# Transposing V on VectorE in a decode attention block with gradients: 32x32 blocks, block-diagonal score weights, and small products on ScalarE

## Chip, cores, metric

One Trainium2 chip, one core. The metric is the device time of that core in microseconds, as the median of several executions. An execution over 1.5% above the fastest of its kernel counts as slow, the others as fast. Engines: PE is the matrix engine, PEld its weight loads, DVE is VectorE, ACT is ScalarE, POOL is GpSimd, SP issues the transfers (SPq is its queue).

## The reference

A decode block for one token, forward and backward: layer norm, attention over a cache (32 query heads, 32 KV heads, 8192 positions, 128 per head), plus a gated MLP. Outputs are the block's output and the gradients of x, both caches and all weights.

```python
q = (xn @ wq).reshape(B, Sq, Hq, Dh)                      # xn = layernorm(x); D = 640
scores = jnp.einsum("bhqd,bhkd->bhqk", q, k) * Dh ** -0.5
p = softmax(scores)
o = jnp.einsum("bhqk,bhkd->bhqd", p, v)
out = x + o.reshape(B, Sq, Hq * Dh) @ wo + (silu(xn @ w1) * (xn @ w3)) @ w2
# ... outputs: out, and jax.vjp(...)(grad_out): dx, dK, dV, dwq, dwo, dw1, dw3, dw2
```

Per head the kernel loads K and V (2 MB each) and stores dK and dV (2 MB each): 32 heads are 268 of the 303.5 MB that are moved. dV is the outer product of p with the row `do` = wo·g, and dK the outer product of U = p·(do·V + const) with q. So a head needs the scores q·K, the softmax, then do·V, then a dot product, and only then may dK be formed.

## The kernel before

One head, in the order in which the instructions are issued. `T` transposes a 128x512 fp32 piece (pairs of bf16 taken as one fp32) with four PE transposes and copies it out of PSUM on ACT. `Mp` takes the score sums from two such pieces. `ev` and `selm` bring the sums to positions on partitions.

```python
def T(h, kind, c):
    W3 = kv_tiles[(kind, h)][:].bitcast(F32).rearrange("p (i w) -> p i w", w=P)
    pT = pst()
    for k in range(4):
        nc.tensor.transpose(pT[:, k * P:(k + 1) * P], W3[:, 4 * c + k, :], ident_f[:])
    KT = kt_tile()
    nc.scalar.copy(KT[:].rearrange("p k w -> p (k w)"), pT[:])
    hd[h]["kt"][(kind, c)] = KT

def Mp(h, kind, c0):
    # ... 4 matmuls, weights 128x32 (one column tile for each piece), 128x512 moving

def head(h):
    # ...
    if has_prev:
        outers_a(h - 1)          # V: two outer products, store dV; K: the first half
    for c in range(had, NCH, 2):
        T(h, "K", c); T(h, "K", c + 1)
        if c >= 2: Mp(h, "K", c - 2)
        # ...
    T(h, "V", 0); T(h, "V", 1)
    Mp(h, "K", NCH - 2); ev(h, "K")
    T(h, "V", 2); T(h, "V", 3)
    selm(h, "K"); mx(h)          # row maximum over 64 positions (DVE)
    # ... further V pieces between: mx_bc (maximum over partitions), expo, zsum
    probs(h)                     # 1/sum, P2 (DVE), Z (DVE)
    if has_prev:
        outers_b(h - 1)          # K: the second half, store dK
    # ... T(h, "V", 7), side work, weights and rows of head h + 1
    T(h + 1, "K", 0); T(h + 1, "K", 1)
    Mp(h, "V", NCH - 2); ev(h, "V")
    o_sum(h)                     # 16 matmuls p·V
    selm(h, "V"); rdot(h)        # dot product on DVE
    T(h + 1, "K", 2)
    dsum(h)                      # its broadcast by PE, then U2 and Z on DVE
    T(h + 1, "K", 3); Mp(h + 1, "K", 0)
    dq_sum(h)                    # 16 matmuls U·K
```

Loads and stores share one queue, in program order; ten buffers of 2 MB rotate. A store gives its buffer back and at once asks for the next load, which goes out only with three buffers free:

```python
def load_next():
    if not pending or len(free_slots) < lag[0]:      # lag[0] = 3 after the start
        return
    kind, h = pending.pop(0)
    t = free_slots.pop(0)
    fifo(t[:], (kc if kind == "K" else vc)[h])        # nc.sync queue
    # ...
def store(kind, h):
    t = kv_tiles.pop((kind, h))
    # ...
    fifo((dkc if kind == "K" else dvc)[h], t[:])
    free_slots.append(t)
    load_next()
```

The MLP is computed between heads 1 and 2. While it runs, K and V of heads up to 5 are asked for.

## Time and profile before

| | before |
|---|---|
| time, median of 3 | 730.84 us (730.36 to 731.22) |
| span of the profiled run, mean granted PE clock | 729.3 us, 0.928 |
| moved | 303.5 MB, 416 GB/s over the span |

The first part of the page gives each engine's busy time and share of the span; the fourth, the chain of work that ended last, followed back from the last instruction and summed by engine.

```profile
PE 600.8 (82%) x5186; PEld 375.4 (51%) x5193; DVE 461.3 (63%) x811; ACT 375.8 (52%) x727; POOL 28.2 (4%) x43
...
DMA 55%; PE 34%; DVE 6%; ACT 2%; issue 1%; SPq 0%; ACTq 0%; DVEq 0%
```

PE is the busiest engine, but more than half of the chain lies in transfers. That, and the full DMA row which the prediction quotes, make this a kernel at the DMA's limit with an engine not far below it.

### The profile page before, as it was taken

To read this page: it belongs to the slowest core of one execution; us is meant where nothing else is said; L and a number is where in the kernel's file an instruction comes from. 1 tells how busy PE (TensorE), PEld (TensorE's weight loads), DVE (VectorE), ACT (ScalarE), POOL (GpSimd) and SP (SyncE) were. 2 spreads that over 40 slices of the span, in tenths; PEclk is the share of its full clock that TensorE was granted. 3 is DMA by queue.
4 is the path that set the end of the run, shared out by engine and by line. 5 is a ranking of instruction groups with operands and counts; after the bars stand their busy time and mean duration, and the time that the engine had idled before them with its cause. 6 is when DMAs were issued, how large, how long until landed. Compare 5 with 4: busy or idle time off the path is not lost.

```text
span 729.3 us, 12905 instructions
## 1 busy us (share of the span) xinstructions
PE 600.8 (82%) x5186; PEld 375.4 (51%) x5193; DVE 461.3 (63%) x811; ACT 375.8 (52%) x727; POOL 28.2 (4%) x43
## 2 busy tenths in 40 slices
PE   4989589999999989887897798877897878977930
PEld 2556366665566556554454454544564545544520
DVE  4179646677868886676466755655746765667482
ACT  3740736665666566554465554554564555645510
POOL 0010100000100000001000000000000000000000
PEclk9996799999999999999999999998999999999965
DMA  8999999999999999999999999999999999999994
GB/s 353 404 411 422 427 427 428 417 426 426 414 417 426 430 426 426 428 428 428 422 428 430 428 425 428 427 428 429 424 429 425 430 429 430 428 427 430 430 396 161
DMA packets 28005, 303.53 MB, mean 416 GB/s; under 512 B 2804, under 2 KB 5304, under 8 KB 11304
## 3 DMA queue, kind: packets, MB, share of 16 engines
q1 hardware_dynamic: 22518, 277.70, 90.1%
q0 software_dynamic: 5408, 24.99, 8.4%
q8 instruction: 41, 0.67, 0.4%
q14 instruction: 20, 0.16, 0.1%
q10 hardware_dynamic: 18, 0.01, 0.0%
HBM read 151.34 MB, written 151.34 MB: 415 GB/s over the span
## 4 chain that ended last, share of the span: by engine, by line
DMA 55%; PE 34%; DVE 6%; ACT 2%; issue 1%; SPq 0%; ACTq 0%; DVEq 0%
DMA kv<-in_A_v_cache_dram 21%; DMA out_dram<-kv 18%; PE pT L318 16%; DMA kv<-in_A_k_cache_dram 14%; PE sA L339 5%; PE dA L339 3%; PE X L433 3%; DVE kv L466 3%; PE m L356 2%; DMA wo_g<-in_A_wo_dram 2%; PE gu_ps L556 1%; ACT KT L320 1%; PE dh_ps L567 1%; DVE wq_g L521 1%; PE acc L199 1%
## 5 line engine op out<-in xcount | busy, mean ns | idle before, releaser
L320 ACT COPY KT<-pT 128x512 f32<-128x512 f32 x512 | 287.9, 587 | 230.0 <-PE pT L318 210.3
L318 PE MATMUL pT<-ident_f,kv 128*128 128x128 f32 x2048 | 306.0, 288 | 62.5 <-DMA kv<-in_A_k_cache_dram 35.3
L318 PEld LDWEIGHTS pT<-ident_f,kv 128*128 128x128 f32 x2048 | 235.4, 148 | 155.1 <-PE pT L318 50.0
L466 DVE TENSOR_TENSOR kv<-qd,U 128x4096 bf16<-128x4096 bf16 x64 | 146.1, 2285 | 0.0
L466 DVE TENSOR_TENSOR kv<-qd,P 128x4096 bf16<-128x4096 bf16 x64 | 143.6, 2285 | 0.0
L433 PE MATMUL X<-kv,Z 128*32 128x512 bf16 x1024 | 95.2, 407 | 1.8 <-DVE Z L450 1.8
L339 PE MATMUL dA<-KT,qz 128*32 128x512 bf16 x512 | 83.5, 405 | 0.0
L339 PE MATMUL sA<-KT,qz 128*32 128x512 bf16 x512 | 83.5, 406 | 0.0
L416 DVE SCALAR_TENSOR_TENSOR U<-m,P 128x64 bf16<-128x64 f32 x32 | 7.5, 234 | 87.2 <-PE m L356 87.2
L382 DVE TENSOR_REDUCE mrow<-m 128x1 f32<-128x64 f32 x32 | 7.2, 224 | 69.6 <-PE m L356 69.5
L433 PEld LDWEIGHTS <-Z 128*32 128x32 bf16 x1024 | 33.0, 100 | 34.5 <-issue 7.1
L339 PEld LDWEIGHTS <-qz 128*32 128x32 bf16 x1024 | 29.6, 95 | 40.5 <-issue 38.0
L356 PE MATMUL m<-selc,KT 64*128 64x64 f32 x256 | 30.5, 242 | 7.9 <-ACT KT L346 7.8
L356 PEld LDWEIGHTS m<-selc,KT 64*128 64x128 f32 x256 | 21.5, 144 | 29.9 <-ACT KT L346 20.0
L376 ACT CAST qd<-pT 128x256 bf16<-128x256 f32 x32 | 11.9, 372 | 40.3 <-DVE kv L466 31.6
L389 DVE TENSOR_REDUCE negM<-m 128x1 f32<-128x128 f32 x32 | 9.3, 292 | 33.0 <-PE m L386 33.0
L521 DVE SCALAR_TENSOR_TENSOR wq_g<-wq_g,side 128x512 bf16<-128x512 bf16 x40 | 27.3, 683 | 0.0
L257 DVE SCALAR_TENSOR_TENSOR side<-wo_g,g_bc 128x640 bf16<-128x640 bf16 x32 | 26.2, 820 | 0.7 <-DMA wo_g<-in_A_wo_dram 0.3
L448 DVE SCALAR_TENSOR_TENSOR U<-m,P 128x128 bf16<-128x128 f32 x32 | 11.4, 355 | 16.4 <-PE m L446 16.4
L406 DVE RECIPROCAL rZ<-m 128x1 f32<-128x1 f32 x32 | 5.3, 167 | 24.1 <-PE m L400 24.1
L346 ACT COPY KT<-dA 64x512 f32<-64x512 f32 x32 | 18.6, 582 | 2.9 <-PE dA L339 2.9
L346 ACT COPY KT<-sA 64x512 f32<-64x512 f32 x32 | 18.5, 579 | 2.0 <-PE sA L339 1.7
(161 smaller groups left out, 372.2 us busy)
## 6 DMA issues: line engine op xcount, KB each, us to landing
out_dram<-kv SPq DMA_DIRECT2D x64, 2048.0 KB, 31.0
kv<-in_A_k_cache_dram SPq DMA_DIRECT2D x32, 2048.0 KB, 26.3
kv<-in_A_v_cache_dram SPq DMA_DIRECT2D x32, 2048.0 KB, 26.3
wq_g<-in_A_wq_dram POOLq DMA_DIRECT2D x7, 640.0 KB, 13.4
wo_g<-in_A_wo_dram POOLq DMA_DIRECT2D x7, 640.0 KB, 19.1
out_dram<-wo_g POOLq DMA_DIRECT2D x7, 640.0 KB, 11.9
out_dram<-wq_g POOLq DMA_DIRECT2D x7, 640.0 KB, 13.4
kv<-in_B_w_dram SPq DMA_DIRECT2D x2, 1728.0 KB, 29.2
```

The source lines that it names most:

```text
L257: nc.vector.scalar_tensor_tensor(junk[:], G_["wo"][:, hh, :], 1.0, g_bc[:], ALU.mult, ALU.mult, accum_out=G_["do"][:, hh:hh + 1])
L318: nc.tensor.transpose(pT[:, k * P:(k + 1) * P], W3[:, 4 * c + k, :], ident_f[:])
L320: nc.scalar.copy(KT[:].rearrange("p k w -> p (k w)"), pT[:])
L339: nc.tensor.matmul(S_[kind][q:q + QW, :], lhsT=S_["qz"][:, o:o + QW], rhs=KTb[c][:, par, :], start=(c0 == 0 and par == 0), stop=(c0 == NCH ...
L346: nc.scalar.copy(XS[0:QH].rearrange("p k w -> p (k w)"), S_.pop(kind)[0:QH, :])
L356: nc.tensor.matmul(S_["m"][:, b0:b0 + 4 * J].rearrange("p (x c k t) -> p k x c t", x=4, k=4, t=2)[:, k], lhsT=XS[0:QH, k, :], rhs=selc[0:Q ...
L376: nc.scalar.copy(qd[:].rearrange("p a d -> p (a d)"), hd[h].pop("ps_r"))
L389: nc.vector.tensor_reduce(S_["negM"][:], S_["m"][:, 2 * J:2 * J + P], AX.X, ALU.max, negate=True)
L433: nc.tensor.matmul(xg["X"][q:q + QW, :], lhsT=Z[:, o:o + QW], rhs=W[:, N4 * i:N4 * (i + 1)], start=(slot == 0 and i < 4), stop=(slot == NS ...
L448: nc.vector.scalar_tensor_tensor(S_["U2"][:], S_["V"][:, 0:J].unsqueeze(2).to_broadcast([P, J, 2]), S_["m"][:, OC + NS:OC + NS + 1], S_["P ...
L466: nc.vector.tensor_tensor(dst[:, lo * DH:hi * DH].rearrange("p (j a b) -> p j a b", a=DH // 2, b=2), vec.rearrange("p (a b) -> p a b", b=2 ...
L521: nc.vector.scalar_tensor_tensor(wq_g[:, ci, :], wq_g[:, ci, :], 1.0, dqb, ALU.mult, ALU.mult, accum_out=dxa[:, ci, g:g + 1])
```

## The change

Its intent: PE and ACT carry V's transposes; VectorE has time to spare. So V is transposed by VectorE itself, straight from the loaded buffer, in 32x32 blocks (`TV`). Since the four 32-row blocks then stand apart, the sums need weights in four diagonal blocks, at full width (`MV`), and their result is transposed back by VectorE (`TD`). To make room, VectorE's small products go to ScalarE, and the order is rebuilt: the second K outer product (`outers_b`) behind all V transposes, the wo and wq gradients of a group on ScalarE in a place of their own (`side_a`), the column sums of a group (`col`) in the next head.

```diff
+    def TV(h, c):
+        W = JV * DH // 2
+        VT = kt_tile()
+        nc.vector.transpose(VT[:].rearrange("p k w -> p (k w)"),
+                            kv_tiles[("V", h)][:].bitcast(F32)[:, W * c:W * (c + 1)])
+        hd[h]["vt"][c] = VT
+
+    def MV(h, c):
+        # ...
+        for par in range(2):
+            o = QV + 16 * par - 2 * c
+            nc.tensor.matmul(S_["Vps"][:], lhsT=S_["qv"][:, o:o + P], rhs=VTb[:, par, :],
+                             start=(c == 0 and par == 0), stop=(c == NV - 1 and par == 1), skip_group_check=True)
+
+    def TD(h):
+        V = kt_tile()[:].rearrange("p k w -> p (k w)")
+        nc.vector.transpose(V, S_.pop("Vps")[:])
+        # ... one add of the two halves, into S_["V"]
...
-        nc.vector.tensor_scalar(P2[:], S_["E"][:].unsqueeze(2).to_broadcast([P, J, 2]), rZ[:], None, ALU.mult)
-        nc.vector.tensor_copy(Z_vals, P2[:, :, 0].rearrange("p (i r) -> p i r", r=4))
+        nc.scalar.activation(P2[:], S_["K"].unsqueeze(2).to_broadcast([P, J, 2]), ACTF.Copy, scale=rZ[:])
+        nc.scalar.copy(Z_vals, P2[:, :, 0].rearrange("p (i r) -> p i r", r=4))
...   (the same for Z from U2, the weight fills, and:)
-            nc.vector.tensor_scalar(G_["wo"][:, hh, :], g_bc[:], G_["od"][:, hh, 0:1], None, ALU.mult)
+            nc.scalar.activation(G_["wo"][:, hh, :], g_bc[:], ACTF.Copy, scale=G_["od"][:, hh, 0:1])
-        nc.vector.tensor_scalar(wq_g[:, ci, :], dqb, xn_col[:, ci:ci + 1], None, ALU.mult)
+        nc.scalar.activation(wq_g[:, ci, :], dqb, ACTF.Copy, scale=xn_col[:, ci:ci + 1])
...   (head(h), its new order; side work cut)
+        Mp(h, NCH - 2); ev(h); selm(h); mx(h); side_k(h); mx_bc(h); expo(h)
+        if h > 0 and h % GH == 0:
+            col(h // GH - 1, hd[h]["m"])
+        TV(h, 0); TV(h, 1); side_m(h); MV(h, 0); zsum(h)
+        TV(h, 2); MV(h, 1); TV(h, 3); probs(h); MV(h, 2); TV(h, 4); MV(h, 3)
+        side_a(h)
+        TV(h, 5); MV(h, 4); TV(h, 6); MV(h, 5); TV(h, 7); MV(h, 6); MV(h, 7)
+        fill_qz(h + 1)
+        outers_b(h - 1)
+        o_sum(h, 0, NI // 2)
+        T(h + 1, 0); T(h + 1, 1)
+        TD(h); rdot(h); dsum(h)
+        o_sum(h, NI // 2, NI)
+        u2(h)
+        T(h + 1, 2); T(h + 1, 3); Mp(h + 1, 0)
+        dq_sum(h)
```

(The head's lines are joined here with semicolons.)

## The prediction

> **What bounds the kernel now.** I read first the slices of the page, then the table of busy time by stage, the waits of the DMA-issuing queue, and the order in time of one head.
>
> ```profile
> DVE  4179646677868886676466755655746765667482
> PEclk9996799999999999999999999998999999999965
> DMA  8999999999999999999999999999999999999994
> GB/s 353 404 411 422 427 427 428 417 426 426 414 417 426 430 426 426 428 428 428 422 428 430 428 425 428 427 428 429 424 429 425 430 429 430 428 427 430 430 396 161
> ...
> HBM read 151.34 MB, written 151.34 MB: 415 GB/s over the span
> ```
>
> From the second slice to the last but two the 16 DMA engines are never below 0.9, at 425 to 430 GB/s once the MLP's weights are in. 303.5 MB (the page's total) at 428 GB/s is 709 us of the 729.3. What is left is the first slice (353 GB/s) and the end (396 and 161). So nothing done on the engines can win more than those 20 us.
>
> Does compute feed the transfers with room to spare? These are the queue's own waits, first for 100 to 250 us, then for 250 to 480 us:
>
> ```profile
> SPq L105 <- DVE kv L466: 60.8, 8, 13.4
> SPq L105 <- DMA out_dram<-kv: 60.6, 8, 15.1
> ```
> ```profile
> SPq L105 <- DMA out_dram<-kv: 206.3, 21, 12.3
> ```
>
> In the first stretch the queue waits half for outer products (stores not ready: compute is catching up after the MLP), in the second for a buffer's store to land. Ordered by time, the K loads are issued every 21.36 us (286.50 to 649.66 in 17 heads): the DMA's pace per head, group weights included. While compute catches up (115 to 243 us in the chain that ended last) it needs 18 us per head, so 3.4 us of every head are slack later. That slack is what the change may spend.
>
> ```profile
> L320 ACT COPY KT<-pT 128x512 f32<-128x512 f32 x512 | 287.9, 587 | 230.0 <-PE pT L318 210.3
> L318 PE MATMUL pT<-ident_f,kv 128*128 128x128 f32 x2048 | 306.0, 288 | 62.5 <-DMA kv<-in_A_k_cache_dram 35.3
> L466 DVE TENSOR_TENSOR kv<-qd,U 128x4096 bf16<-128x4096 bf16 x64 | 146.1, 2285 | 0.0
> L466 DVE TENSOR_TENSOR kv<-qd,P 128x4096 bf16<-128x4096 bf16 x64 | 143.6, 2285 | 0.0
> L416 DVE SCALAR_TENSOR_TENSOR U<-m,P 128x64 bf16<-128x64 f32 x32 | 7.5, 234 | 87.2 <-PE m L356 87.2
> L382 DVE TENSOR_REDUCE mrow<-m 128x1 f32<-128x64 f32 x32 | 7.2, 224 | 69.6 <-PE m L356 69.5
> ```
>
> PE and ACT carry the catch-up, through transposes and their copies; DVE waits for their results (157 us in the last two rows). Half of the 2048 transposes and 512 copies are V's.
>
> [...] The trace before has no such instruction. [...] 683 ns for the 128x512 SCALAR_TENSOR_TENSOR. Consecutive VectorE instructions of the trace overlap by 80 ns (two outer products take 4.49 us, not 4.57), so I take 620 ns from start to start. Fp32 at half this rate is the chief doubt. [...] the trace's plain PSUM copies take 587.
>
> **The change, part by part.**
>
> VectorE, summed busy time. Removed: P2 (10.5 us), two Z copies (6.3, 6.8), the weight fill (5.4), dwo (10.2), dwq (14.1): 53 us. Added: 8 V transposes in each of 32 heads, 256 x 0.69 = 177; 32 transposes of the sums, 22; 32 small adds, 7; four more mask products for each of 8 groups, 6: 212. 461 becomes about 620 us, 85%.
>
> PE loses V's 1024 fp32 transposes (about 150 us of the 306) and the 128 V selection matmuls; the V score matmuls stay at 16 per head, now full width. They lose the overlap of column tiles, and cost about 0.21 us each (four consecutive full-width matmuls of the query row start within 0.65 us): 3.4 us per head, against 8 x 0.59 = 4.7 for the transposes alone. ACT loses 256 copies and 32 evictions (about 162 us) and takes over the small products: per head P2, two Z copies, three fills, a share of dwo and dwq[...]. Both get lighter. All this lies beside the DMA; only the pace per head matters.
>
> VectorE's pace per head, as it issues in order: four outer products, 4 x 2.2 = 8.8; eight V transposes, 5.0; transpose of sums, add, dot product and U2, 0.65 + 0.3 + 0.3 + 0.4; waiting for the dot product's broadcast, 0.5 (0.48 in the trace); row maximum and its broadcast, 0.55, with 1.03 of waiting where no side work fills it; reciprocal 0.2. For the row maximum it waits about 0.3: before, K's sums were ready 7.7 us after U2 with V transposes among them, now about 1.5 us sooner, while three outer products last 6.6. These sum to 18.0. Side work is uneven: 0.2 in the first head of a group, about 2.25 in the second (three dx products of 0.75), 2.4 in the third, 3.6 in the fourth; in the last three, some 0.75 of it fills the 1.03 of waiting. That gives 18.2, 19.5, 19.6 and 20.8, mean 19.5 us. It is more than the 18 of now, and 1.8 under the DMA's 21.36. So the DMA goes on setting the pace. A V transpose could take 0.62 + 1.8/8 = 0.85 us before VectorE does.
>
> Where is the slack thin? After the MLP. By 121.46 us, where head 2's V store is issued, I count 50.75 MB issued, and the stages before sum to 49.7 MB moved: only about 1 MB, 3 us of work, is outstanding. That store comes at the same time after the change: head 2's K part ends about 1.6 us sooner, its eight transposes and the sums end near 117, and two outer products later it is 121.3. But head 2's K store came 9.3 us later (130.75). Now its second outer product stands behind all V transposes of head 3, the heaviest in its group: 2.2 + 0.55 + 0.9 + 0.65 + 5.0 + 1.9 + 0.2 + 0.8 + 2.2 = 14.4 us. In it the DMA has 1 MB + a store + a load = 5.2 MB, 12.2 us: about 2.2 us idle, once. From head 4 the group weights raise the DMA's need above VectorE's pace, and a cushion grows.
>
> The end. K of the last head lands at 676, V at 686.1. Then before: transposes, sums, U2 at 696.5, outer products until 705.4, weight gradients until 713.0. After: U2 of head 30 comes 2 us sooner, its outer products end near 684.8, the maximum of head 31 near 685.6; eight transposes end at 692.4, the last K outer product at 694.6, the sums and U2 at 696.8. dwo and dwq run on ACT beside dx and end about 0.3 us sooner. Nothing in sum. Heads 0 and 1 reach the MLP at about the same time (head 0 sooner, head 1 as slow).
>
> Sum: 730.8 + 2.2 + 0 = 733.
>
> **Rivals.** (1) VectorE becomes the bound. For it: 85% busy over the span, in-order waits on three PE results per head, and an instruction that the trace never timed. Against it: 1.8 us of slack. At 0.9 us per transpose the pace is 21.7 and the time about 730.8 + 30 x 0.4 + 2 = 745; at 1.2 us (half rate) it is 24.1, and about 815. (2) It gets faster, because PE and ACT no longer limit the catch-up. For it: 230 us of ACT waiting for transposes. Against: the DMA row is full in just that stage, so a shorter chain hands the queue transfers it can't take. A win could only come from the last 40 us: 727 at best. (3) The early gap is hidden (more outstanding than I count) or grows, since full-width sums, the burst of dwo on ACT, or four shared KT buffers delay head after head: 730.5 or 738.
>
> **Range and chances.** The centre is 733. The low end, 727, is no gap and a shorter end. The high end, 752, lets VectorE exceed the DMA's pace by 0.7 us. Faster by over 2% needs 716, 7 us above the pure transfer time: 0.03. Slower by over 2% (745.5) needs transposes beyond 0.9 us or stalls that I don't see: 0.17. The rest, 0.80, is within 2%.
>
> **What would show it.** V's transposes of 128x512 at 0.66 to 0.72 us each, starting 0.62 apart. VectorE near 85%, PE near 70%, ACT near 40%. The DMA row still at 9 throughout, with a dip near 133 us. K loads 21.3 us apart after 300 us, the queue waiting there for stores to land; if it waits for outer products there, rival 1 holds. The prediction is wrong if transposes exceed 0.85 us, or if the row maximum or the sums wait over 2 us per head on PE.

Passages are cut from the recorded text, and marked there, because no trace or run of this case shows them. No term of the time is among them: its sum stays 730.8 + 2.2 + 0 = 733 us. Four notes on what is left:

- "Such instruction" is a transpose on VectorE.
- The 0.69 us for one V transpose, and the 620 ns from start to start, are estimates. What the trace before shows for them is the 683 ns of a 128x512 SCALAR_TENSOR_TENSOR and the overlap of 80 ns: 683 - 80 = 603. That fp32 might take twice as long was a doubt, which that trace neither shows nor excludes.
- ACT's "near 40%" counted in a figure for the small products. In the trace after they took 94 us (P2, Z, fills, dwo and dwq of the page by forms), against 53 on VectorE before.
- The "overlap of column tiles" is in the trace before: four score matmuls with 128x32 weights take 0.64 us together (316.82 to 317.46) at about 0.4 each, and 512 of them keep PE busy for 83.5 us, 0.16 each.

## The result, and the profile after

| | before | after |
|---|---|---|
| median of 6 runs each | 730.75 us (729.71 to 731.72) | 736.04 us (734.96 to 737.71) |
| span of the profiled run, mean granted PE clock | 729.3 us, 0.928 | 733.4 us, 0.852 |

The ratio is 1.0073, interval 1.0057 to 1.0089: within 2%, and surely a little slower. (A ratio is the mean time of one kernel's fast runs over the mean of the other's of the same rounds, so not quite the ratio of the medians quoted.) The results are correct.

From the page of the changed kernel: the busy times, then rows of the 40 slices, then the chain that ended last.

```profile
PE 581.9 (79%) x4073; PEld 306.5 (42%) x4073; DVE 596.2 (81%) x968; ACT 298.2 (41%) x703; POOL 28.3 (4%) x43
...
DVE  4489658888887997888887898888897888788882
...
PEclk9898799998898898988898898888898898888975
DMA  9999999999999999999999999999999999999984
GB/s 352 400 410 423 426 428 427 366 428 421 427 420 430 426 429 427 424 429 430 426 423 430 428 430 428 426 425 431 428 425 426 432 425 429 432 426 431 426 344 154
...
PE 55%; DVE 27%; ACT 7%; issue 6%; DMA 4%; ACTq 0%; DVEq 0%
```

Three things are to be seen. VectorE went from 63 to 81% and is now the busiest. The DMA row still stands at 9 up to the last two slices: by that row nothing changed, except one slice of 366 GB/s (the eighth, 128 to 147 us) and the last but one, 344 for 396. But the chain has turned over: DMA 55% became 4%. A full DMA row and a chain without DMA in it go together here, and which of the two to believe is the lesson.

The groups that answer to those of before (busy time, mean ns of one, idle time before, releaser):

```profile
L373 PE MATMUL dA<-KT,qv 128*128 128x512 bf16 x512 | 184.0, 494 | 30.0 <-DVE KT L362 29.8
L340 ACT COPY KT<-pT 128x512 f32<-128x512 f32 x256 | 138.4, 590 | 97.9 <-PE pT L338 97.4
L362 DVE STREAM_TRANSPOSE KT<-kv 128x512 f32<-128x512 f32 x256 | 164.5, 684 | 10.8 <-PE m L500 6.1
...
L424 DVE TENSOR_REDUCE mrow<-m 128x1 f32<-128x64 f32 x32 | 7.2, 225 | 62.9 <-PE m L396 62.9
L418 ACT CAST qd<-pT 128x256 bf16<-128x256 f32 x32 | 11.8, 368 | 78.5 <-DVE kv L506 72.7
```

The V transposes take 684 ns, as estimated. They wait for almost nothing. VectorE's one large wait is the row maximum's, 62.9 us in 32 heads; 17.4 of it lies in the three heads up to the MLP, the rest is 1.57 us per head in the 29 after it.

The queue's own waits, of the changed kernel, 100 to 250 us:

```profile
SPq L105 <- DVE kv L506: 118.3, 13, 13.5
SPq L105 <- DMA out_dram<-kv: 19.6, 3, 14.9
```

and 250 to 480 us:

```profile
SPq L105 <- DVE kv L506: 133.1, 21, 11.9
SPq L105 <- DMA out_dram<-kv: 82.9, 18, 9.6
```

Before, the second stretch had no wait for outer products at all; now the queue waits there 133 us for them and 83 for landings. From 480 to 680 us it is mostly landings again (153.7 against 23.5), but that doesn't say that compute is ahead: no PE or VectorE instruction of a head waits for a load in this run.

### Where the time came from

In every head the last thing before the outer products of dK is the product U2 (the row of VectorE with the 128x128 result). I take its time in head 2, the first after the MLP, and in head 31, the last, and what remains to the end of the run. "Pace" is the difference over 29 heads. The table holds every profiled run whose profile is fast and whose end was not reordered:

| kernel | U2 of head 2 | U2 of head 31 | pace | profiled time | time - last U2 |
|---|---|---|---|---|---|
| before | 116.45 | 696.14 | 19.99 | 731.02 | 34.9 |
| after | 115.59 | 703.02 | 20.26 | 735.14 | 32.1 |
| e1, third K piece earlier | 117.40 | 694.74 | 19.91 | 732.89 | 38.2 |
| e3, K outer product early | 115.76 | 713.03 | 20.60 | 745.17 | 32.1 |
| e4, a ninth transpose | 117.99 | 727.45 | 21.02 | 759.68 | 32.2 |
| e5, one transpose | 114.17 | 690.10 | 19.86 | 728.68 | 38.6 |
| e11, before with small products on ACT | 116.65 | 753.28 | 21.95 | 785.44 | 32.2 |
| e12, third qd buffer | 115.68 | 703.23 | 20.26 | 735.34 | 32.1 |
| e13, e1 and e12 | 115.86 | 693.93 | 19.93 | 732.56 | 38.6 |

The last column falls into two kinds. Either it is 32.1 to 32.2, whatever the kernel: then the computing chain sets the end. Or it is 35 to 39: then head 31 was ready earlier than the transfers behind it, and the DMA sets the end, at 729 to 733 us. A kernel with the 32.1 reaches before's 731.0 if its last U2 comes at 698.9, that is at a pace of (698.9 - 115.6) / 29 = 20.1 us. The changed kernel runs at 20.26: 0.15 x 29 = 4.3 us too late, which is the difference of the profiled runs (4.1).

The queue's own waits near the end tell the two kinds apart. In the changed kernel (700 to 725 us) the longest in sum is for outer products; in the kernel before (696 to 721 us) it is for older stores to land:

```profile
SPq L105 <- DVE kv L506: 13.9, 2, 7.9
```
```profile
SPq L105 <- DMA out_dram<-kv: 25.0, 4, 11.1
```

In the same 25 us, e3, e4, e11 and e12 wait for outer products too, and e1, e5 and e13 for stores to land.

So the DMA's 21.36 us per head is not what compute has to keep under. After the MLP compute is behind: when head 2's U2 comes, at 115.6 us, the loads of heads 3, 4 and 5 have all been issued (the last at 107.6). At the end it has to be level with the last load. 21.36 - 20.1 = 1.3 us per head, 36 us over 29 heads, are the arrears to be made up. Three other traces bear the sum out, by when PE first waits for a load again: in before at 302 us, after ten heads at 17.9 us (35 us made up); in e5 at 398, after 14 heads at 19.0 (33 us); in e1 at 550, after 21 heads at 19.7 (35 us). The changed kernel's 29 heads at 20.26 make up 32, too few. From 284.9 to 645.4 us its K loads were issued 21.2 us apart while its heads took 20.5: compute was gaining on the loads, but too slowly. The changed kernel never once waits for a load in the heads after that (before: 62.5 us on PE, 35.3 of them for K, in the row quoted in the prediction), and the heads run strictly in fours: 20.9, 19.2, 19.6, 22.3 us, from head 8 to head 29.

Where the pace is lost, in the third head of a group (VectorE, in order of time: start, duration, and in brackets the idle time before and its releaser):

```profile
256.86 0.35 DVE L489 SCALAR_TENSOR_TENSOR U<-m,P 128x128 bf16<-128x128 f32 x1 [0.48 <-PE m L484]
257.13 4.48 DVE L506 TENSOR_TENSOR kv<-qd,P 128x4096 bf16<-128x4096 bf16 x2
261.53 2.28 DVE L506 TENSOR_TENSOR kv<-qd,U 128x4096 bf16<-128x4096 bf16 x1
265.05 0.23 DVE L424 TENSOR_REDUCE mrow<-m 128x1 f32<-128x64 f32 x1 [1.23 <-PE m L396]
```

and PE at the same time:

```profile
256.75 0.62 PE L475 MATMUL X<-kv,Z 128*32 128x512 bf16 x8
257.30 1.09 PE L338 MATMUL pT<-ident_f,kv 128*128 128x128 f32 x8
...
258.57 1.26 PE L475 MATMUL X<-kv,Z 128*32 128x512 bf16 x13
259.76 1.09 PE L338 MATMUL pT<-ident_f,kv 128*128 128x128 f32 x8
260.79 0.63 PE L355 MATMUL sA<-KT,qz 128*32 128x512 bf16 x4
261.35 1.09 PE L338 MATMUL pT<-ident_f,kv 128*128 128x128 f32 x8
262.37 1.46 PE L355 MATMUL sA<-KT,qz 128*32 128x512 bf16 x8
264.56 0.46 PE L396 MATMUL m<-selc,KT 64*128 64x64 f32 x4 [0.72 <-ACT KT L388]
```

VectorE has three outer products to do from U2 on, until 263.8. In that time PE has to finish p·V, transpose the six K pieces left, take U·K and K's sums: by the trace it is busy without a pause from 256.75 to 263.8, then ACT copies the sums (0.72) and PE selects (0.46), and VectorE has waited 1.23 us. From U2 to the row maximum it is 8.2 us; the prediction had set 7.7 - 1.5 = 6.2 for K's sums, and so 0.3 of waiting.

In the last head of a group it is 2.78 us, because PE's granted clock was halved (0.50) in just that place (timeline of the changed kernel, PE, then windows of 1 us; columns of the latter: us, busy time of PE, PEld, DVE, ACT, POOL, granted clock, DMA share, GB/s):

```profile
276.32 0.62 PE L475 MATMUL X<-kv,Z 128*32 128x512 bf16 x8
...
278.45 2.32 PE L475 MATMUL X<-kv,Z 128*32 128x512 bf16 x14
```
```profile
277.00:278.00 1.00, 1.00 (x8) 0.72 (x8) 1.00 (x1) 0.68 (x2) 0.00 (x0) 0.85 1.00 414
278.00:279.00 1.00, 1.00 (x13) 0.46 (x16) 1.00 (x2) 0.73 (x2) 0.00 (x0) 0.50 1.05 434
279.00:280.00 1.00, 1.00 (x14) 0.33 (x8) 1.00 (x1) 0.00 (x0) 0.00 (x0) 0.50 1.05 446
```

The U·K matmuls take 2.32 us where they took 1.26 in the head before. In the first head of a group the column sums, now in that head, stand on PE ahead of VectorE: the fourth V transpose waits 1.15 us for them.

The early gap was there too: the slice of 366 GB/s. Summed from windows of 10 us, the changed kernel had moved 0.49 MB less than before by 140 us, 1.05 less by 150, and from then to 700 us about 0.85 less: 2 us of transfer, at 133 us, as predicted.

### The profile page after: what moved, and what is told of

Same layout as the page of the kernel before. It is cut to its first block, busy times and chain, and to the rows that moved or that the text cites. A ratio compares the mean times of both kernels' runs of the same rounds, so it can differ in the third digit from the quotient of the medians.

```text
span 733.4 us, 10753 instructions
## 1 busy us (share of the span) xinstructions
PE 581.9 (79%) x4073; PEld 306.5 (42%) x4073; DVE 596.2 (81%) x968; ACT 298.2 (41%) x703; POOL 28.3 (4%) x43
## 4 chain that ended last, share of the span: by engine, by line
PE 55%; DVE 27%; ACT 7%; issue 6%; DMA 4%; ACTq 0%; DVEq 0%
PE pT L338 15%; PE sA L355 11%; PE dA L373 8%; PE X L475 8%; DVE kv L506 8%; DVE KT L362 8%; DMA kv<-in_A_v_cache_dram 3%; DVE wq_g L561 3%; ACT KT L388 3%; PE m L396 2%; DVE KT L379 2%; PE m L500 2%; PE m L484 2%; ACT wq_g L567 2%; PE pT L270 1%
## 5 line engine op out<-in xcount | busy, mean ns | idle before, releaser
L373 PE MATMUL dA<-KT,qv 128*128 128x512 bf16 x512 | 184.0, 494 | 30.0 <-DVE KT L362 29.8
L340 ACT COPY KT<-pT 128x512 f32<-128x512 f32 x256 | 138.4, 590 | 97.9 <-PE pT L338 97.4
L362 DVE STREAM_TRANSPOSE KT<-kv 128x512 f32<-128x512 f32 x256 | 164.5, 684 | 10.8 <-PE m L500 6.1
L338 PE MATMUL pT<-ident_f,kv 128*128 128x128 f32 x1024 | 144.7, 286 | 0.0
L338 PEld LDWEIGHTS pT<-ident_f,kv 128*128 128x128 f32 x1024 | 113.8, 144 | 55.8 <-PE X L475 14.8
L373 PEld LDWEIGHTS <-qv 128*128 128x128 bf16 x512 | 58.9, 126 | 97.6 <-issue 82.4
L424 DVE TENSOR_REDUCE mrow<-m 128x1 f32<-128x64 f32 x32 | 7.2, 225 | 62.9 <-PE m L396 62.9
L418 ACT CAST qd<-pT 128x256 bf16<-128x256 f32 x32 | 11.8, 368 | 78.5 <-DVE kv L506 72.7
L355 PEld LDWEIGHTS <-qz 128*32 128x32 bf16 x512 | 20.1, 95 | 35.1 <-issue 29.8
L484 PE MATMUL m<-rdot,masks 128*128 128x1 f32 x64 | 12.2, 260 | 27.1 <-DVE U L457 27.1
L449 ACT ACTIVATE P<-m,rZ 128x128 bf16<-128x128 f32 x32 | 11.6, 363 | 53.1 <-DVE rZ L447 53.1
L396 PE MATMUL m<-selc,KT 64*128 64x64 f32 x128 | 14.6, 234 | 23.2 <-ACT KT L388 23.2
L396 PEld LDWEIGHTS m<-selc,KT 64*128 64x128 f32 x128 | 10.2, 137 | 39.5 <-ACT KT L388 39.5
```

Source lines behind the costliest of these rows:

```text
L355: nc.tensor.matmul(S_["K"][q:q + QW, :], lhsT=S_["qz"][:, o:o + QW], rhs=KTb[c][:, par, :], start=(c0 == 0 and par == 0), stop=(c0 == NCH ...
L362: nc.vector.transpose(VT[:].rearrange("p k w -> p (k w)"), kv_tiles[("V", h)][:].bitcast(F32)[:, W * c:W * (c + 1)])
L373: nc.tensor.matmul(S_["Vps"][:], lhsT=S_["qv"][:, o:o + P], rhs=VTb[:, par, :], start=(c == 0 and par == 0), stop=(c == NV - 1 and par == ...
L396: nc.tensor.matmul(S_["m"][:, 0:4 * J].rearrange("p (x c k t) -> p k x c t", x=4, k=4, t=2)[:, k], lhsT=XS[0:QH, k, :], rhs=selc[0:QH].rea ...
L484: nc.tensor.matmul(S_["m"][:, OC + NS:OC + NS + 1], lhsT=negones_b, rhs=S_["rdot"][:], start=False, stop=True, skip_group_check=True)
```

## The experiments

Twelve kernels ran; a thirteenth build failed. Each ran beside the kernel before on the same chip, whose medians were 730.0 to 731.0. All results are correct but e5's.

### e1: the third K piece of the next head ahead of the sums

If the row maximum waits because PE has too much between U2 and K's sums, one transposition group earlier should shorten it.

```diff
             T(h + 1, 0)
             T(h + 1, 1)
+            T(h + 1, 2)
         TD(h)
@@ after u2(h)
-            T(h + 1, 2)
             T(h + 1, 3)
```

> Theory A (compute lag): after the MLP the changed kernel is one chain of compute at 82.0 us per four heads that never waits for a load; it ends as late as its last U2 (703.0 us) plus the rest. One transpose group of the next head's K moved ahead of the dot product's broadcast takes some 0.5 us per head out of the way from U2 to the row maximum: the wait before the row maximum falls from 1.24 to about 0.7 us, the period to about 80 us, the last U2 to about 696 where loads bind again, the time to 732 to 733. Theory B (only the gap at 133 to 150 us counts, 0.9 MB = 2.1 us, because 20.5 us per head is under the DMA's 21.36): 736, unchanged.

Measured: 731.65 us (730.65 to 732.89, 5 runs), ratio to before 1.0005 (0.9992 to 1.0018). The row maximum's waits, and the queue's in 250 to 480 us:

```profile
L424 DVE TENSOR_REDUCE mrow<-m 128x1 f32<-128x64 f32 x32 | 7.2, 225 | 41.4 <-PE m L396 41.4
```
```profile
SPq L105 <- DMA out_dram<-kv: 150.3, 19, 12.3
SPq L105 <- DVE kv L506: 58.3, 13, 10.0
```

62.9 became 41.4 us. In the 29 heads after the MLP it is 0.79 us in every head, where it had been 1.23 in most and 2.8 in the last of a group. Heads 8 to 23 ran at 19.63 us where the changed kernel takes 20.49. From 550 us on PE waits for K loads again, so over all 29 heads the pace fell by 0.35 only, to 19.91, and the loss is gone within the noise. This is the chief evidence: one line moved, no instruction removed, and the wait that was mis-sized carried the time. What is not separated is the clock: the mean granted clock rose with it, from 0.85 to 0.90 in 250 to 578 us.

### e2 and e12: a third buffer for the rows q and do

ACT waits 72.7 us in the changed kernel, to write rows for the next head into a buffer that outer products still read. A rival: this wait, by way of the weight fills and the PSUM copies behind it on ACT, delays K's sums.

```diff
-        qd = small.tile([P, 2, DH], BF16, name="qd")
+        qd = small.tile([P, 2, DH], BF16, name="qd", bufs=3)
```

As e2 this did not build: it needed 3.125 KB per partition where 2.78 were left. e12 is the same with the scratch of the last few instructions moved into a used buffer.

> The run that did not build for want of SBUF, mended: a third buffer for the row qd (some end-of-kernel scratch moved to a shared buffer to make room). ScalarE then no longer waits (72.7 us in all) for the second K outer product before it copies the next head's first K groups. If this wait is what delays those copies and with them the row maximum: its wait falls from 1.24 to 0.5 to 0.8 us, mean pace from 20.26 to under 19.9 us, last U2 near 695, 731 to 733 us. If the copies are held up by PE alone: 736, pace unchanged.

Measured: 737.20 us (735.34 to 738.63, 4 runs), ratio 1.0104 (1.0088 to 1.0121).

```profile
L424 DVE TENSOR_REDUCE mrow<-m 128x1 f32<-128x64 f32 x32 | 7.2, 225 | 65.9 <-PE m L396 65.9
...
L418 ACT CAST qd<-pT 128x256 bf16<-128x256 f32 x32 | 11.6, 362 | 15.3 <-PE pT L412 15.2
```

ACT's wait fell from 78.5 to 15.3 us and nothing followed: the row maximum waits as before, the pace is 20.26 to the digit. This large wait did not lie on the path, and was worth nothing.

### e13: both

```diff
+ e1's lines and e12's lines
```

> The third qd buffer and the third K group early together. Either one brings the last U2 to where loads bind, so together they should win nothing more: 730 to 732 us, last U2 not before 692. If the pace still mattered below the break-even of 20.0 us per head, it would be 728 or less.

Measured: 732.56 us (731.58 to 733.76, 5 runs), ratio 1.0035 (1.0022 to 1.0049). Nothing more was won, as expected, though the time is just above my 730 to 732. Pace 19.93, as e1 alone. Under 20.1 (19.86 to 19.99 in before, e1, e5 and e13) the DMA sets the end and the engines have nothing more to win.

### e3: the K outer product early again

The change had moved `outers_b` behind all V transposes; this puts it back behind `probs`, to fill the gap at 133 us.

```diff
         probs(h)
+        if has_prev:
+            outers_b(h - 1)
         MV(h, 2)
@@ after fill_qz(h + 1)
-        if has_prev:
-            outers_b(h - 1)
         o_sum(h, 0, NI // 2)
```

> The second K outer product goes back to where it stood, right after the probabilities. K stores come about 5 us sooner. Theory B: the gap between 133 and 150 us goes, 0.9 MB = 2.1 us won: 734. Theory A: the gap goes, but the time follows the period of four heads: ScalarE's wait for the product goes too (as in the run with a third qd buffer), while the sums now wait about 1 us for the last V score matmuls: period 80 to 83 us, time 732 to 737.

Measured: 748.54 us (745.17 to 752.86, 6 runs), ratio 1.0244 (1.0220 to 1.0268). My 732 to 737 was missed. The gap did go (430 and 424 GB/s in 120 to 140 and 140 to 160 us, for 408 and 390 in the changed kernel). But nothing now stands between the last V transpose and the transposition of the sums:

```profile
L379 DVE STREAM_TRANSPOSE KT<-dA 128x512 f32<-128x512 f32 x32 | 22.9, 717 | 33.0 <-PE dA L373 33.0
```

33.0 us of waiting where the changed kernel has 4.8. In return the row maximum waits 52.6 us instead of 62.9, because the 2.8 of a group's last head are gone. In heads 8 to 23 nothing is lost in sum: both kernels take 20.49 us per head (82 for four, within the 80 to 83 expected). The 10 us of the profiled runs (745.17 against 735.14) come from elsewhere: 2.5 us in heads 3 to 7, and 7.5 from head 24 on. Why the last heads are slower is not settled; in 600 to 620 us the granted clock was 0.76, against 0.83 in the changed kernel. So closing the gap won nothing here, but the run doesn't show that the outer product's late place is the better one in a steady head.

### e4: a ninth transpose

If VectorE's row sets the pace, 0.61 us more in it costs 29 times as much; if there is slack up to the DMA's 21.36, nearly nothing.

```diff
         hd[h]["vt"][c] = VT
+        if c == 4:
+            nc.vector.transpose(VT[:].rearrange("p k w -> p (k w)"),
+                                kv_tiles[("V", h)][:].bitcast(F32)[:, W * c:W * (c + 1)])
```

> One V transpose per head done twice (into the same tile, result unchanged): 0.62 us more on VectorE per head. Theory A (no slack left): 29 heads x 0.62 = 18 us, 754 us, period 84.5 us. Theory B (0.9 us of slack under the DMA's pace): 736 to 738.

Measured: 755.64 us (754.90 to 759.68, 4 runs), ratio 1.0350 (1.0329 to 1.0372): theory A. The pace rose by 0.76, more than the 0.61 added (why is open), and 0.76 x 29 = 22 us, against 24.5 between the profiled runs and 19.6 between the medians. In 250 to 480 us the queue now waits for outer products alone:

```profile
SPq L105 <- DVE kv L509: 208.5, 22, 14.6
```

A pace of 21.0 is still under the DMA's 21.36, and it costs 20 us. That settles that 21.36 was the wrong limit.

### e5: one V transpose instead of eight

Seven are left out and the first one's result is used in their place, so do·V and the gradients built on it are wrong.

```diff
         W = JV * DH // 2
+        if c:
+            hd[h]["vt"][c] = hd[h]["vt0"]
+            return
         VT = kt_tile()
+        hd[h]["vt0"] = VT
```

> Wrong result on purpose: only the first of a head's eight V transposes is done, and all eight pairs of score matmuls read it. Seven times 0.61 = 4.3 us less on VectorE per head. Theory A (VectorE's pace ends the run, break-even at 20.0 us per head): pace well under 20.0, VectorE or PE waits for loads again after some 250 us, last U2 near 692 to 696, 729 to 732 us, no lower, because the DMA then sets the end. Rival (PE at its lower granted clock, with full-width score matmuls, sets the pace): 735 to 736 as before, period still about 82 us per four heads.

Measured: 728.48 us (728.37 to 728.68, 4 runs), ratio 0.9965 (0.9951 to 0.9978). From head 4 on, heads take 17.2 to 19.7 us while compute catches up; from 398 us on loads bind ("some 250 us" was expected):

```profile
PE pT L338 <- DMA kv<-in_A_k_cache_dram: 28.3, 11, 3.5
```

With 4.2 us per head taken off VectorE the kernel is 2.3 us faster than before, just below the 729 to 732 expected. So almost nothing was to be won: with V's transposes on VectorE nearly free, and this order and end, the time is 728.5. PE's mean clock was low here too (0.876, with the same full-width matmuls), so that rival alone doesn't explain the changed kernel's pace.

### e6: e1, with the gap and the end treated

The K outer product early in head 3 alone, where the gap arises, and at the end the column sums' results (`fin_od`, `fin_pe`) ahead of the last K outer products, so that the weight gradients are ready sooner.

```diff
+ e1's lines
-        if has_prev:
+        if has_prev and h != 3:
             outers_b(h - 1)
@@ after probs(h)
+        if h == 3:
+            outers_b(h - 1)
@@ the end
     outers_a(H - 1)
-    outers_b(H - 1)
     fin_od(NG - 1)
     fin_pe(NG - 1)
+    outers_b(H - 1)
     fin_wo(NG - 1)
```

> A version that should beat both: the third K group early (as in the run that gave 731.65), the K outer product early in head 3 alone, and at the end the last group's output gradients worked out between the K outer products instead of after them. Theory A: the dip at 133 to 150 us mostly goes (deficit in bytes at 150 us against the kernel before under 0.8 MB instead of 1.77), the last U2 is near 692 to 695, and the stores of dwo and dwq start 2 to 4 us sooner after it: 722 to 727 us. If the gap and the end don't matter: 731 to 732.

Measured: 732.95 us (732.32 to 734.49, 5 runs), ratio 1.0031 (1.0017 to 1.0045). My 722 to 727 was missed. The gap moved rather than closed: the bytes moved lagged before's by 0.30 MB at 150 us, but by 1.38 at 170. At the end dwo was ready at about 706 us and the last dK store had been issued at 705.48, but dwo's store was issued only at 712.48. In between the one queue stood still for 6.6 us. Its own waits in 704 to 716 us put that down to the landing of a small output row, of which dwo's store needs no data and which the program stores later, so what it truly waited for stays open:

```profile
SPq L105 <- DMA out_dram<-KT: 6.9, 2, 6.6
```

### e7: the kernel before with that end

```diff
+ the lines of e6 under "the end", in the kernel before
```

> The kernel before with only the new order at the end. It is bound by loads until 686 us, so the end is all compute and stores: U2 at 696 stays, dwo and dwq are stored 1 to 3 us sooner: 727 to 730 us. It tells how much of the new version's gain is owed to the change (if it gives as much, none).

Measured: 730.25 us (730.07 to 730.89, 5 runs), ratio 0.9991 (0.9978 to 1.0003): the same, at the edge of the 727 to 730 expected. The order at the end is worth nothing by itself.

### e8: the small products back on VectorE

Undoes one part of the change: P2, both Z, the fills, dwo and dwq.

```diff
-        nc.scalar.activation(P2[:], S_["K"].unsqueeze(2).to_broadcast([P, J, 2]), ACTF.Copy, scale=rZ[:])
+        nc.vector.tensor_scalar(P2[:], S_["K"].unsqueeze(2).to_broadcast([P, J, 2]), rZ[:], None, ALU.mult)
... the same for the other five
```

> The changed kernel with all its small products (P2, both Z copies, the weight fills, dwo, dwq) back on VectorE. By the rows of before these are 1.4 to 1.6 us per head. Theory A (no slack): 29 heads x 1.5 = 43 us, 775 to 785 us, period near 88 us. If VectorE's waits (1.24 us before the row maximum, 0.48 before U2) can take them up, 736 to 750.

Measured: 777.79 us, median of the three fast runs (773.82 to 780.72), ratio 1.0634 (1.0598 to 1.0670). The fourth, profiled run, 794.86, counts as slow, so its trace is not compared. 775 to 785 was expected: with these products on it, VectorE's row grows by some 1.4 us per head (41.8 us between the medians of fast runs, over 29 heads). The move is what makes V's transposes affordable.

### e11: only the small products on ScalarE, in the kernel before

The other half: does the move help by itself, without V's transposes and without the new order?

```diff
-        nc.vector.tensor_scalar(P2[:], S_["E"][:].unsqueeze(2).to_broadcast([P, J, 2]), rZ[:], None, ALU.mult)
+        nc.scalar.activation(P2[:], S_["E"][:].unsqueeze(2).to_broadcast([P, J, 2]), ACTF.Copy, scale=rZ[:])
... the same for the other five, order unchanged
```

> The small products alone moved to ScalarE, V still transposed on TensorE. VectorE loses 53 us of work that lay beside the DMA, ScalarE gains some 80. Theory A (only a pace above the break-even of 20.0 us per head costs time): catch-up pace 18 to 19.5 us, 730 to 732 us, the same as before. If ScalarE becomes the bound: over 735.

Measured: 785.13 us (784.76 to 786.10, 4 runs), ratio 1.0740 (1.0726 to 1.0755). 730 to 732 was missed by far.

```profile
ACT wq_g L523 <- DVE wq_g L521: 108.4, 35, 6.5
...
DVE mrow L382 <- PE m L356: 143.7, 32, 10.4
```

dwq's product on ACT must wait until VectorE has read the same rows of wq for dx, which stands behind outer products. The PSUM copies stand behind it in ACT's order, PE waits for those (67.2 us in all), and the row maximum for PE: two heads of four take 26.7 and 24.2 us, the others 17.7 and 20.1. This chain is read from the trace; no run removes it alone. In the change, `side_a` puts these products where their inputs are ready. The move and the reordering are one thing; the first without the second costs 54 us.

### e9 and e10: the last two stores from another queue

dwo and dwq of the last group from ACT's queue, with e6's end; e9 on e1, e10 on the kernel before.

```diff
-        for lo, hi in ((0, 60), (60, P)):
-            fifo(dst[lo:hi], t[lo:hi])
+        nc.scalar.dma_start(dst, t[:])
```

> The changed kernel with the third K group early, the new order at the end, and the last dwo and dwq stores issued from ScalarE's queue, since in the last runs they stood behind the K and V stores in the one queue until 712 us though dwo was ready at 706. If that queue's order sets the last 15 us: 722 to 727 us. If the drain of the last stores does, whatever queue they come from: 730 to 732.

> The same end on the kernel before: dwo and dwq are ready 1 to 3 us later there, because VectorE makes both. If the queue's order sets the end: 723 to 728 us; else 730.

Measured: e9 731.25 us (730.06 to 732.30, 5 runs), ratio 1.0000 (0.9986 to 1.0014); e10 732.47 us (732.14 to 733.38, 5 runs), ratio 1.0020 (1.0006 to 1.0034). In e9 dwo was issued at 706.09 and dwq at 709.84 us, 5 and 3 us sooner than in e1. But the queue's waits of e9 from 690 us on show that the trial was spoiled by longer waits:

```profile
SPq L105 <- DMA out_dram<-kv: 24.7, 1, 24.7
SPq L105 <- DMA out_dram<-wo_g: 11.3, 1, 11.3
```

The main queue first waited 24.7 us for an older store to land, then 11.3 us for dwo itself, and issued the last three K and V stores at 705.87, 717.60 and 718.04 us (e1: 695.88, 701.15, 706.08). In e10 the first of these three went out at 706.33. No data asks for these waits; what imposes them I don't know, and shorter ones of the kind are in e6 and e1 too. The transfers stood at 227 and 190 GB/s in 700 to 704 and 704 to 708 us, and made up for it with 414 and 438 in 720 to 724 and 724 to 728, where e1 has 176 and 66. This suggests, without proving it, that in the kernels with the old queue the poor rate of the last 12 us belongs to the dwo and dwq stores that stand last, since K and V stores in the same place ran at over 400 GB/s. Whether the end can be shortened by placing them in between, without these waits, stays open.

## Why the prediction was right

733.0 was predicted and 736.0 measured, in the range of 727 to 752 and within 2%. By its steps:

- **Transposes: right.** 690 ns each, 620 from start to start, were estimated; 684 and about 600 (four start within 1.80 us, from 269.07 to 270.87) came out, and 709 for the 32 transposes of the sums, which read PSUM. Rival 1's half rate (1.2 us) is excluded. ScalarE's products of 512 and 640 elements took 711 and 820 ns in the trace.
- **Busy shares: VectorE 85% predicted, 81% measured; ACT 40 and 41; PE 70 and 79.** PE's miss is the V score matmuls: 0.21 us each by the spacing of the query row's matmuls, but 184.0 us busy for 512 in the trace, 0.36 each. The mean granted clock fell from 0.928 to 0.852.
- **Pace: mis-sized by 0.8.** 18.2, 19.5, 19.6, 20.8, mean 19.5, were summed; the steady groups run at 20.9, 19.2, 19.6, 22.3, mean 20.5, and all 29 heads at 20.26. The term at fault is "for the row maximum it waits about 0.3": it waits 1.24 us in most heads and 2.8 in the last of a group, since half of p·V, U·K and six K pieces don't fit under three outer products, least of all where the clock is halved (0.50 from 278 to 281 us). In the first head of a group the column sums on PE add about 1.9 (1.15, 0.30 and 0.45 in waits), which the prediction didn't count. The middle two came out right because other terms were about 1 us too large. e1 shows the row maximum's part by taking most of it away.
- **Criterion: wrong.** "1.8 under the DMA's 21.36. So the DMA goes on setting the pace", and the threshold of 0.85 us per transpose drawn from it, failed. The limit is 20.1, as compute starts behind the loads and must end level with them. By the predicted pace there would still have been 0.6 of slack, so the verdict held; with the measured pace it was 0.15 over. e4 shows it: at 21.0 us, inside the supposed slack, 20 us are lost. By the prediction's own signs rival 1 held in part: the queue did wait for outer products (133.1 us in 250 to 480, against 82.9 for landings), although the K loads came 21.2 us apart, as predicted. Its other sign of being wrong, over 2 us of waiting on PE per head, was met only in the last head of a group (2.8; 1.57 on average). Rival 1's sum for 0.9 us per transpose (745) used the same wrong limit; from 20.1 it would have been 730.8 + 29 x 1.6, some 777.
- **The gap near 133 us: right in size, but not what the time is made of.** 2.2 us predicted, 0.85 MB or 2 us measured. e1 has a larger one, yet its median is 0.7 us above that of before: it is 1.5 MB behind in bytes moved (summed as above) from 200 to 650 us, and about 0.1 MB at 730. Before leaves the last two slices of the DMA partly empty (396 and 161 GB/s), and what was lost early is moved there. So the 2.2 of "730.8 + 2.2 + 0" should have been 0, and its 0 for the end should have been about 4: the last U2 came at 703.0, not 696.8 (696.1 in before), and what follows it took 32.1, not 34.9.
- **No gain: right, and for the reason given** in rival 2. e5, at 728.5, shows how little was to be won.

The right total is in part luck: the measured pace was over the limit that the prediction had not seen, but only by 0.15 us, and a counted 2.2 that cost nothing stood for an uncounted 4.3.

What stays open: whether full-width weights lower PE's granted clock (it was 0.876 in e5 with the same matmuls and 0.919 in e11 without them, which goes with it but proves nothing); what halved the clock (it was 0.50 from 268 to 270 and from 278 to 281 us; PE's longest pause between 248 and 288 us was 1.83 us); and the end of the run. No version with correct results was clearly faster than the kernel before: e1 (731.65) and e9 (731.25) equal it.

## What to carry to other kernels

With loads issued well ahead, the full DMA row (9 up to the last two slices) did not say here that compute had slack: compute that started behind its loads had to make up the arrears as well, so the pace that it had to hold was shorter than the DMA's time per head (20.1 us against 21.36; at 21.0, in e4, 20 us were lost). Look at whether the chain that ended last holds the DMA or the engines, and at what comes after the last head: a remainder that was the same in kernels of different speed (32.1 to 32.2 us here) went with an end set by the engines. When work moves to another engine, what stands behind it there in program order decides: the same products on ScalarE cost 54 us in the old order and made the change possible in the new one.
